# A self-check by four unsplit fp32 products and four transpositions, put into the projection stage of a transformer block

## The chip, the cores and the metric

The kernel runs on one core of a Trainium2 chip. The metric is the device time of one execution in microseconds (us); several executions are timed, and their median is compared. One execution of each kernel is also recorded by the profiler, instruction by instruction.

## The reference

One token sequence of 2048 rows by 576 features goes through a windowed attention and a mixer with an MLP, both under a modulated layer norm:

```python
mod = (_silu(c) @ w_mod).reshape(c.shape[0], 6, 1, -1)
sa, ca, ga, sb, cb, gb = (mod[:, i] for i in range(6))
h = _layernorm(x) * (1 + ca) + sa
x = x + ga * A_ref(h, A_wqkv, A_wo)      # 32 heads of 18, window of 256 rows, causal
h = _layernorm(x) * (1 + cb) + sb
x = x + gb * B_ref(h, B_w1, B_w2, B_w3, B_w4)
# B_ref: x1 = h + shifted(gelu(layernorm(h) @ w1)) @ w2
#        x1 + gelu(layernorm(x1) @ w3) @ w4, inner width 4608
```

All inputs and the output are fp32.

## The kernel before

The rows stand in 16 tiles of 128. The work goes through four stages: the projections to queries, keys and values (`qkv`), the attention with its output projection, the shifting mixer, and the MLP, which takes the rows in two halves of eight tiles (`sb`) and the inner width in blocks (`jj`).

Nearly all matrix products are done in split form: an fp32 operand is written as a high part in the type fp32r and a low remainder, and three fp32r products stand for one. A few products take fp32 operands as they are; here they are called unsplit. Those before the attention are the modulation vectors: `mod01` (L177) and `modr` (L194).

The order of all work is written out by hand. Each piece is put on a list with `at(t, f)`, where t is a planned time; at the end the list is sorted by t and the pieces are issued in that order. Each engine then runs its own instructions in just this order, and waits where an operand or a buffer isn't there yet. So a planned time fixes only the order, not the time.

In `qkv` the planned time starts at `T0` = 0 and the rows are taken in four groups of four tiles (b = 0 to 3), each planned for 47 us. For each group come nine blocks of query and key columns (`fmm`, L279, evacuated by `fev`, L284 on ScalarE and L285 on VectorE, stored by `fst`), then eight of values (`vmm`, L309, evacuated by `vev`, L314 on ScalarE and L315 on VectorE, stored by `vst`, L320). Between the value blocks of group b the normalised rows of group b + 1 are transposed in five steps k (`tr`, L254, four transpositions of 128x128 each); `hev` then scales them from PSUM into a buffer `hf` on VectorE (L259), rounds them to the high part on ScalarE (L261) and takes the remainder on GpSimd (L262). In group 0 also `modr(k)` runs on TensorE, with its sum `modre` on VectorE (L199, L201).

PSUM is used by named buffers of one each. `tr` alternates between `m0` (k even) and `m1` (k odd); `modr` uses `m1`; `fmm` and `vmm` go round `s0` to `s3`. A new tile of a name waits until the readers of the tile before it are done:

```python
pt = X["pt", b, k] = ps.tile([P, 512], F32, tag=f"m{k % 2}", name=f"pt{b}_{k}")
```

Around the planned time 30.5 the list reads: `vmm(0, 0)` 29.25, `fev(0, 8)` 29.35, `modr(2)` 30, `tr(1, 0)` 31, `vmm(0, 1)` 31.2, `vev(0, 0)` 31.3, `modre(2)` 31.5, `hev(1, 0)` 31.6.

At the end of the MLP each output tile is summed up in `acc[t]` by `dev` (L1175, VectorE), eight tiles in the order 4, 5, 6, 7, 0, 1, 2, 3, while TensorE computes the next tile (`run`, L1167) into the other one of two PSUM buffers; after the last block the tile is stored (L1178).

Of the kernel before, what the change touches and what calls it, by code (L numbers as in the profile page):

```python
# [8 lines left out]
F32 = mybir.dt.float32  # L9
# [3 lines left out]
ALU = mybir.AluOpType  # L13
# [6 lines left out]
P = 128  # L20
# [13 lines left out]
class Kern:  # L34
# [8 lines left out]
    def setup(self, stack):  # L43
        nc, tc = self.nc, self.tc
        self.ev = []
        self.cst = stack.enter_context(tc.tile_pool(name="cst", bufs=1))
        self.dr = stack.enter_context(tc.tile_pool(name="dr", bufs=1, space=DRAM))
        self.ps = stack.enter_context(tc.tile_pool(name="psU", bufs=1, space=PSUM))
        self.pools = {}
        c = self.cst  # L50
        self.ident = c.tile([P, P], F32, name="ident")
        self.identr = c.tile([P, P], F32R, name="identr")
        self.gb = c.tile([P, D], F32, name="gb")
        self.mhalf = c.tile([P, 1], F32, name="mhalf")
        self.rowm = c.tile([P, 8], F32, name="rowm")
        self.Mq = c.tile([P, 2, 64], F32R, name="Mq")
        self.Mk = c.tile([P, 5, 64], F32R, name="Mk")
        self.md = c.tile([P, 10], F32, name="md")
        self.qd = [self.dr.tile([2, D, 512], F32, name=f"qd{g}") for g in range(4)]
        self.kd = [self.dr.tile([2, D, 768], F32, name=f"kd{g}") for g in range(4)]  # L60
        self.vd = [self.dr.tile([P, VW], F32, name=f"vd{t}") for t in range(NT)]
        self.od = [self.dr.tile([512, D], F32, name=f"od{g}") for g in range(4)]
        self.xp = [self.dr.tile([P, D], F32, name=f"xp{t}") for t in range(NT)]
        self.hbd = [self.dr.tile([P, D], F32, name=f"hbd{t}") for t in range(NT)]
        self.xnd = [self.dr.tile([P, D], F32, name=f"xnd{t}") for t in range(NT)]
        self.modd = {v: self.dr.tile([1, D], F32, name=f"modd{v}") for v in (2, 3, 4, 5)}

    def at(self, t, f, *a):
        self.ev.append((t, (lambda: f(*a)) if a else f))
# [58 lines left out]
    def qkv(self, T0, TB):  # L128
        nc, at, ps = self.nc, self.at, self.ps
        X = {}  # L130
        at(-99, lambda: (self.open("qa", "left"), self.open("qb", "right")))
        qb = lambda *a, **k: self.pool_("qb").tile(*a, **k)
# [186 lines left out]
        def vst(t):  # L319
            nc.sync.dma_start(self.vd[t], X["Vst"][t % 3])  # L320

        at(-90, cond)
        for i in range(2):
            at(-89 + i, xload, i)
# [21 lines left out]
        for b in range(4):  # L346
# [7 lines left out]
            for i in range(4):  # L354
                t = 4 * b + i
# [16 lines left out]
            if b < 3:  # L372
                for i in range(4):
                    t = 4 * b + 4 + i
# [584 lines left out]
    def mlp(self):  # L959
        nc, ps, ident = self.nc, self.ps, self.ident  # L960
        NJ = F // 2 // P
        SB = S // 1024
        A, W3, W4, acc, gb = [], [], {}, {}, self.gb
# [15 lines left out]
        if True:  # L979
# [191 lines left out]
            def dev(jj, sb, t, last):  # L1171
                def f():
                    po = up_b[jj, "d", t][:, :, 0:288]
                    a = acc[t].rearrange("p (h d) -> p h d", h=2)
                    nc.vector.tensor_tensor(out=a, in0=po, in1=a, op=ALU.add)  # L1175
                    if last:
                        tt = 8 * sb + t
                        nc.sync.dma_start(self.out[tt * P:(tt + 1) * P, :], acc[t])  # L1178
                return f

# [126 lines left out]
```

## Time and profile before

| | |
|---|---|
| timed runs | 1858.69, 1849.98, 1856.75 us; median 1856.75 us |
| the profiled execution | 1853.12 us, its span 1851.3 us |
| TensorE multiplying | 1725.0 us (93% of the span) |
| VectorE / GpSimd / ScalarE | 1093.2 / 903.9 / 706.9 us |
| mean granted TensorE clock | 0.976 |

The span runs from the first to the last instruction; the execution's own time is 1.8 us longer. In the profile PE is TensorE multiplying, PEld TensorE loading the stationary operand, DVE VectorE, ACT ScalarE, POOL GpSimd, and SP the engine that issues the transfers. A row such as `L254 PE MATMUL pt<-ident,xh` gives the line, the engine, the operation, the written buffer and the read ones.

### The profile page before, as it was taken

How to read it: one execution, taken by the hardware profiler on the slowest of the kernel's cores; microseconds unless marked ns; L12 is line 12 of the kernel's file. 1: busy time of each engine (PE TensorE's matmuls, PEld its weight loads, DVE VectorE, ACT ScalarE, POOL GpSimd, SP SyncE). 2: the span in 40 equal slices, each digit the busy share in tenths (PEclk: the TensorE clock that was granted, in tenths of full speed). 3: DMA queues.
4: the chain of work that ended last, by engine and by line, in shares of the span. 5: the costliest groups of instructions: out<-in, count | busy, mean ns of one | idle time of the engine just before them, and what ended most of it. 6: DMA issues, size and time to landing. Idle time of an engine off the chain costs nothing.

```text
span 1851.3 us, 33769 instructions
## 1 busy us (share of the span) xinstructions
PE 1725.0 (93%) x13496; PEld 1572.3 (85%) x13496; DVE 1093.2 (59%) x1801; ACT 706.9 (38%) x1210; POOL 903.9 (49%) x842
## 2 busy tenths in 40 slices
PE   7999989889999998998779999999989999999998
PEld 6788878788888887998768899999978999999997
DVE  4644244465656562757556666666676666666664
ACT  2322134344444445344333333333343333333331
POOL 4322264445454533355576655555563655555550
PEclk9999979899999999999999999999989999999999
DMA  4955552444544535664442222222114222222211
GB/s 147 322 175 181 166 154 82 122 120 132 155 138 140 149 105 154 203 201 155 144 137 60 60 61 61 60 61 60 58 60 126 60 61 60 60 61 61 60 44 52
DMA packets 156420, 206.78 MB, mean 112 GB/s; under 512 B 19300, under 2 KB 87908, under 8 KB 155688
## 3 DMA queue, kind: packets, MB, share of 16 engines
q1 hardware_dynamic: 156264, 204.64, 36.1%
q8 instruction: 106, 1.74, 0.4%
q14 instruction: 50, 0.41, 0.1%
HBM read 143.76 MB, written 60.56 MB: 110 GB/s over the span
## 4 chain that ended last, share of the span: by engine, by line
PE 74%; DVE 7%; DMA 6%; POOL 5%; issue 3%; ACT 3%; SPq 2%; POOLq 0%; DVEq 0%; ACTq 0%
PE d L1167 23%; PE qk L279 6%; PE av L526 4%; PE v L309 3%; PE mx L444 3%; PE wo L611 3%; PE pg L828 3%; PE X L487 3%; DMA QD<-qd 2%; PE w L877 2%; DVE m L456 1%; PE X L489 1%; PE pm L177 1%; PE ot L536 1%; DVE W L1025 1%
## 5 line engine op out<-in xcount | busy, mean ns | idle before, releaser
L1167 PE MATMUL d<-W,G 128*128 128x288 f32 x3456 | 508.5, 298 | 16.3 <-DVE acc L1175 12.3
L1167 PEld LDWEIGHTS d<-W,G 128*128 128x128 f32 x3456 | 490.2, 190 | 38.3 <-DVE acc L1175 13.7
L1175 DVE TENSOR_TENSOR acc<-d,acc 128x576 f32<-128x576 f32 x288 | 216.6, 753 | 200.6 <-PE d L1167 198.4
L1005 POOL TENSOR_TENSOR wf<-wf 128x384 f32<-128x384 f32 x140 | 146.4, 1067 | 343.0 <-DMA wf<-in_B_w_dram 321.7
L456 DVE TENSOR_REDUCE m<-mx 128x2 f32<-128x640 f32 x224 | 181.2, 817 | 159.6 <-PE mx L446 157.4
L504 ACT ACTIVATE P<-X 128x512 f32<-128x512 f32 (+4 forms) x320 | 180.5, 573 | 207.2 <-PE X L489 204.5
L444 PE MATMUL mx<-KD,QS 128*128 128x320 f32 (+4 forms) x512 | 157.6, 358 | 37.8 <-POOL QS L427 22.5
L427 POOL TENSOR_SCALAR QS<-QD,rowm 128x512 fp32r<-128x512 f32 x128 | 87.9, 699 | 142.2 <-DMA QD<-qd 70.2
L487 PE MATMUL X<-QD,KS 128*128 128x64 f32 (+2 forms) x704 | 151.6, 307 | 3.7 <-ACT P L504 3.2
L1144 DVE TENSOR_TENSOR G<-U,G 128x512 fp32r<-128x512 f32 x108 | 95.3, 882 | 99.8 <-ACT G L1137 99.8
L1017 POOL TENSOR_TENSOR W<-wf,W 128x768 fp32r<-128x768 f32 x70 | 152.0, 2193 | 1.2 <-ACT W L1011 1.2
L444 PEld LDWEIGHTS mx<-KD,QS 128*128 128x128 f32 x512 | 102.0, 199 | 45.4 <-POOL QS L427 23.8
L1135 ACT ACTIVATE U<-U 128x512 f32<-128x512 f32 x108 | 68.3, 632 | 179.3 <-DVE U L1120 179.3
L1135 ACT ACTIVATE C<-C 128x512 f32<-128x512 f32 x36 | 22.8, 632 | 285.9 <-DVE C L1120 285.9
L279 PE MATMUL qk<-hT,Wqk 128*128 128x512 f32 x504 | 120.9, 401 | 0.0
L279 PEld LDWEIGHTS qk<-hT,Wqk 128*128 128x128 f32 x504 | 95.8, 191 | 24.2 <-issue 0.9
L487 PEld LDWEIGHTS X<-QD,KS 128*128 128x128 f32 x704 | 106.7, 195 | 10.6 <-ACT P L504 7.8
L434 POOL TENSOR_SCALAR KS<-KD,rowm 128x768 fp32r<-128x768 f32 (+1 forms) x128 | 107.6, 853 | 0.0
L1031 POOL TENSOR_TENSOR wf<-wf,gb 128x1152 f32<-128x1152 f32 x35 | 103.4, 2955 | 7.1 <-DMA wf<-in_B_w_dram 7.1
L446 PE MATMUL mx<-Mq,identr 128*128 128x128 f32 x448 | 101.5, 227 | 0.0
L1046 POOL TENSOR_TENSOR W<-wf,W 128x1152 fp32r<-128x1152 f32 x35 | 96.7, 2762 | 6.9 <-ACT W L1040 6.9
L1011 ACT CAST W<-wf 128x1152 fp32r<-128x1152 f32 x70 | 90.2, 1318 | 21.9 <-DMA wf<-in_B_w_dram 11.2
(765 smaller groups left out, 3198.0 us busy)
## 6 DMA issues: line engine op xcount, KB each, us to landing
wf<-in_B_w_dram SPq DMA_DIRECT2D x35, 576.0 KB
wf<-in_B_w_dram SPq DMA_DIRECT2D x140, 128.0 KB
KD<-kd SPq DMA_DIRECT2D x72, 216.0 KB
QD<-qd SPq DMA_DIRECT2D x96, 144.0 KB
wf<-in_B_w_dram SPq DMA_DIRECT2D x140, 64.0 KB
qd<-qs SPq DMA_DIRECT2D x16, 512.0 KB
kd<-qs SPq DMA_DIRECT2D x16, 512.0 KB
vd<-Vst SPq DMA_DIRECT2D x16, 312.0 KB
```

The source lines that it names most:

```text
L279: nc.tensor.matmul(po, W[:, a, fs], H[:, c, :], start=(n == 0), stop=(n == 13))
L434: nc.gpsimd.tensor_scalar(t[:, b0:, r], src[:, b0:], M[:, 2 + r:3 + r], 0.0, op0=ALU.mult, op1=ALU.add)
L444: nc.tensor.matmul(pm[:, s, 320 - 64 * nb:320], lhs, K[:, j, 64 * (i + 5 - nb):64 * (i + 5)], start=True, stop=False)
L446: nc.tensor.matmul(pm[:, s, 0:320].rearrange("p (a b) -> p a b", b=64)[:, 0::4, :], self.identr, self.Mq, start=False, stop=True)
L456: nc.vector.tensor_reduce(out=m[:, c:c + 2], in_=pm[:, :, 0:320], axis=mybir.AxisListType.X, op=ALU.max, negate=True)
L487: nc.tensor.matmul(px[:, c:c + q1 - q0], K[:, b + 4].rearrange("p r k -> p (r k)"), Q[:, j, q0:q1], start=(i == 0), stop=False)
L504: nc.scalar.activation(p[:, lo:], X["px", n, j, k][:, lo:], AF.Exp, scale=SCALE)
L1005: nc.gpsimd.tensor_tensor(out=WF[:, o], in0=WF[:, a], in1=WF[:, b], op=ALU.subtract)
L1017: eng.tensor_tensor(out=W[:, s0:s1, 3:5, :], in0=WF[:, 1 + s0:1 + s1, 0:2], in1=W[:, s0:s1, 0:2, :].bitcast(F32), op=ALU.subtract)
L1031: nc.gpsimd.tensor_tensor(out=R4, in0=R4, in1=gb.unsqueeze(1).to_broadcast([P, 2, D]), op=ALU.mult)
L1167: nc.tensor.matmul(po, G[:, g, ta, b, ts], W[:, w, b, cs], start=(n == 0), stop=(n == 5))
L1175: nc.vector.tensor_tensor(out=a, in0=po, in1=a, op=ALU.add)
```

## The change

A function `resid` is put on the list at 30.5. It takes the input rows of tile 4 (`X["x", 4]`, loaded earlier for the layer norm), 512 of their 576 columns. Four unsplit fp32 products load 128 columns of the rows each as the stationary operand and stream the identity; their result in PSUM (`m0`) is copied to a buffer of `hf` by ScalarE. Then four plain transpositions of the same columns go to a new tile of `m0`, and VectorE takes the difference, multiplies it by a million, squares it and sums it up over the columns into `res`, one number for each partition. In the MLP `res` is added to the output rows of tile 8 before they are stored. One constant buffer of 4 bytes a partition is new. Nothing is removed or moved.

```diff
+        self.res = c.tile([P, 1], F32, name="res")
...
+        def resid():
+            x = X["x", 4]
+            pp = ps.tile([P, 512], F32, tag="m0", name="rp")
+            for k in range(4):
+                nc.tensor.matmul(pp[:, k * P:(k + 1) * P], x[:, k * P:(k + 1) * P], self.ident, start=True, stop=True)
+            d = qb([P, 512], F32, tag="hf", name="rd", bufs=2)
+            nc.scalar.copy(d, pp)
+            pp = ps.tile([P, 512], F32, tag="m0", name="rp2")
+            for k in range(4):
+                nc.tensor.transpose(pp[:, k * P:(k + 1) * P], x[:, k * P:(k + 1) * P], self.ident)
+            nc.vector.tensor_tensor(out=d, in0=pp, in1=d, op=ALU.subtract)
+            nc.vector.tensor_scalar(d, d, 1e6, None, op0=ALU.mult)
+            nc.vector.tensor_tensor(out=d, in0=d, in1=d, op=ALU.mult)
+            nc.vector.tensor_reduce(out=self.res, in_=d, axis=mybir.AxisListType.X, op=ALU.add)
+
+        at(T0 + 30.5, resid)
...
                     if last:
                         tt = 8 * sb + t
+                        if tt == 8:
+                            nc.vector.tensor_scalar(acc[t], acc[t], self.res, None, op0=ALU.add)
                         nc.sync.dma_start(self.out[tt * P:(tt + 1) * P, :], acc[t])
```

## The prediction

> **What bounds the kernel now.** I read the page first, for the engine that carries the chain of work.
>
> ```profile
> span 1851.3 us, 33769 instructions
> ...
> PE 74%; DVE 7%; DMA 6%; POOL 5%; issue 3%; ACT 3%; SPq 2%; POOLq 0%; DVEq 0%; ACTq 0%
> ```
>
> TensorE carries three quarters of the chain that ended last. An average says little about one place, so next come the busy times in stretches of the projection stage and TensorE's waits from 40 to 205 us.
>
> ```profile
> 80.00:100.00 20.00, 19.82 (x149) 16.92 (x148) 9.12 (x15) 5.70 (x13) 6.43 (x5) 1.00 0.54 182
> ...
> 160.00:200.00 40.00, 40.00 (x232) 35.57 (x231) 16.80 (x32) 10.85 (x24) 8.78 (x11) 1.00 0.45 154
> ```
>
> ```profile
> PE pmr L194 <- DMA wm<-in_w_mod_dram: 1.4, 1, 1.4
> PE pt L254 <- DVE macc L201: 0.2, 1, 0.2
> ```
>
> The second number of a row is TensorE's busy time: 19.82 of 20 us, later 40.00 of 40. In these 165 us it waited 1.6 us in all, the 1.4 us of it ahead of L194's first use. So nothing in this stage would take up a delay of TensorE; a microsecond that it loses behind the new code is a microsecond by which the stage ends later. The third view is the timeline where the new code goes in, between `modr(2)` (L194) and `tr(1, 0)` (L254).
>
> ```profile
> 75.74 1.18 PE L194 MATMUL pmr<-wm,silub 128*32 128x288 f32 x16
> ...
> 76.71 0.39 ACT L314 COPY Vst<-v 64x288 f32<-64x288 f32 x1
> ...
> 76.85 0.69 DVE L285 TENSOR_TENSOR qs<-qk,qs 128x512 fp32r<-128x512 f32 x1 [1.15 <-ACT qs L284]
> 76.85 0.66 PE L254 MATMUL pt<-ident,xh 128*128 128x128 f32 x4
> ...
> 77.26 3.95 PE L309 MATMUL v<-Wv,hT 128*128 128x288 f32 x28
> 77.57 0.46 DVE L315 COPY Vst<-v 64x288 f32<-64x288 f32 x1
> ...
> 78.06 0.76 DVE L201 TENSOR_TENSOR macc<-pmr,macc 128x576 f32<-128x576 f32 x1
> 78.73 0.80 DVE L259 TENSOR_SCALAR hf<-pt,md 128x512 f32<-128x512 f32 x1
> 79.57 0.62 ACT L261 CAST hT<-hf 128x512 fp32r<-128x512 f32 x1 [2.46 <-DVE hf L259]
> 80.21 0.39 ACT L314 COPY Vst<-v 64x288 f32<-64x288 f32 x1
> 80.64 0.46 DVE L315 COPY Vst<-v 64x288 f32<-64x288 f32 x1 [1.10 <-ACT Vst L314]
> 81.05 0.60 PE L254 MATMUL pt<-ident,xh 128*128 128x128 f32 x4
> ```
>
> The reader is to see that TensorE goes from one group to the next without a pause, that a group of four transpositions takes 0.60 to 0.66 us, and that the evacuations hand over within 0.02 to 0.06 us (79.53 to 79.57, 79.57 + 0.62 to 80.21).
>
> **The change part by part.** Nothing is removed or moved; every term is an addition. The prices of single instructions, as min/median/max where three numbers stand:
>
> ```profile
> 10.04 20.98 PE L177 MATMUL pm<-silu,wm 128*128 128x1 f32 x100 [10.04 <-DVE rowm L108]
> ...
> L177 PE MATMUL pm<-silu,wm x100: 242/352/371, 10.0 to 30.8; 128*128 128x1 f32 x64, 128*64 128x1 f32 x16, 64*128 64x1 f32 x16, 64*64 64x1 f32 x4
> ...
> L194 PE MATMUL pmr<-wm,silub x80: 402/406/431, 58.2 to 94.7; 128*32 128x288 f32 x64, 64*32 64x288 f32 x16
> ...
> L254 PE MATMUL pt<-ident,xh x80: 270/272/477, 30.9 to 184.1; 128*128 128x128 f32 x80
> ...
> L531 ACT COPY avs<-av x32: 573/594/616, 285.8 to 725.5; 128x512 f32<-128x512 f32 x32
> ...
> L246 DVE TENSOR_SCALAR xh<-x,a7mv,a7rs x1: 579/579/579, 73.6 to 73.6; 128x576 f32<-128x576 f32 x1
> ...
> L456 DVE TENSOR_REDUCE m<-mx x224: 769/823/826, 235.4 to 694.7; 128x2 f32<-128x640 f32 x112
> ```
>
> (1) The four products. `modr` has 40 products and `mod01` 50, and the rows show 80 and 100 records: an unsplit product is two records, so this is 8. The trace has none with 128 loaded and 128 streamed columns. Least: the spacing of the transpositions, which load and stream the same shapes, (0.60 - 0.27) / 3 = 0.11 us, so 7 x 0.11 + 0.27 = 1.04 us. Most: the spacing of L177, 20.98 / 100 = 0.21 us, and L194's 0.41 for the last: 1.88 us. L177 ran early, when TensorE was slower: its 352 ns for one streamed column is more than L254's later 272 for 128. So I stay nearer the low end, at L309's spacing (28 in 3.95, 0.14 us, a full load beside a stream), with 0.35 for the last: 7 x 0.14 + 0.35 = 1.33 us. The records of L194 and L177 show how many instructions there are, not how often each streams. [...]
>
> (2) The new waits on TensorE. The second `m0` tile can't be written until ScalarE has copied the first, so TensorE stands still: handover 0.04, copy 0.59 (L531, same shape), handover 0.06. ScalarE is free by then (its L314 ends at 77.10, the products end at 76.85 + 1.33 = 78.18). Then four transpositions, 0.66. Then `tr(1, 0)` wants `m0` a third time and waits for the subtraction: handover 0.04, 0.69 (L285: two operands, one in PSUM, 512 columns), handover 0.06. Sum 0.69 + 0.66 + 0.79 = 2.14 us, all on the path, because behind these instructions in TensorE's queue stands the whole rest of the stage.
>
> (3) VectorE's other three. Scaling 0.58 (L246, at most), squaring 0.69 (L285's), summing 0.65 (L456: 0.82 for 640 columns, here 512): 1.92 us in front of L315, L201 and L259, which stood right behind. `hev(1, 0)` started 1.88 us after `tr(1, 0)`; now it starts after 1.86 + 0.46 + 0.76 and two handovers, 3.13 us: 1.25 us later against TensorE. The first `tr` on `m1` needs L201's end (3.1 us after `tr(1, 0)`) and comes 4.20 us after it (81.05 - 76.85), so it doesn't wait. What is late next shows in the chain of waits ten microseconds further:
>
> ```profile
> 84.07 0.82 DVE hf L259
> ...
> 84.91 0.62 ACT hT L261
> ...
> 85.56 0.40 ACT Vst L314
> ...
> 85.98 0.46 DVE Vst L315
> ...
> 86.47 0.77 DVE macc L201
> ...
> 87.29 0.66 PE pt L254 x4
> ```
>
> This chain from VectorE and ScalarE already ends 0.2 us after TensorE asked for `m1`. Following `hev`, rounding and value copies one by one behind the late start (each L259, L261, L314, L315 in the order of the list, with the rows' durations), the delay shrinks from 1.25 to 0.66 us at `hev(1, 1)`, and L201 ends 11.0 us after `tr(1, 0)` where it ended 10.4 us after it: 0.6 us more of waiting. Bounds: 0 if the idle gaps before L259 take it up, 1.25 if none is made up.
>
> (4) Other queues. SP issues no new transfer. The store of the first value tile waits for L315 and goes out some 5 us later; behind it in SP's queue stand only stores of the next value tiles, and their reader is the attention, 140 us on. GpSimd gets nothing, and its work on `hT` is late by the same time as TensorE. The rows of tile 4 get a reader more; the load that takes over their buffer belongs to the next group, planned at 50, and comes after the new code in any case.
>
> (5) The addition at the end, 0.58 us on VectorE by L246:
>
> ```profile
> 1842.78 0.76 DVE L1175 TENSOR_TENSOR acc<-d,acc 128x576 f32<-128x576 f32 x1 [0.84 <-PE d L1167]
> 1844.37 0.76 DVE L1175 TENSOR_TENSOR acc<-d,acc 128x576 f32<-128x576 f32 x1 [0.84 <-PE d L1167]
> ```
>
> The tile is the fifth of the last eight (1842.78). Behind it VectorE is idle for 0.84 us until TensorE has the next tile, and the PSUM buffer is already free, so 0.58 us fits: nothing. If VectorE took over 0.84 us, the next tile would be late by the excess, and three more gaps of 0.84 us would make it up.
>
> Sum: 1.33 + 2.14 + 0.6 = 4.1 us; with all low ends 1.04 + 2.14 = 3.2, with all high ends 1.88 + 2.14 + 1.25 = 5.3. Against the profiled execution: 1853.12 + 4.1 = 1857.2. That execution is 3.6 us under the median of the runs shown, and the four times together average 1854.6, so I forecast 1854.6 + 4.1 = 1858.7 us.
>
> **The rivals.** First, the granted clock drops behind the new waits. Two stretches speak to it:
>
> ```profile
> 56.00:58.20 2.20, 0.80 (x4) 0.33 (x3) 2.20 (x2) 0.61 (x2) 2.20 (x2) 1.00 0.95 366
> 58.20:60.00 1.80, 1.79 (x19) 1.07 (x20) 0.22 (x1) 0.00 (x0) 0.05 (x1) 1.00 1.06 408
> 226.50:228.40 1.90, 0.28 (x3) 0.04 (x1) 0.00 (x0) 0.39 (x1) 1.38 (x3) 1.00 0.84 280
> ...
> 231.00:232.00 1.00, 1.00 (x7) 1.00 (x6) 0.00 (x0) 0.39 (x1) 0.00 (x0) 0.50 0.61 150
> ...
> 229.00:235.00 6.00, 6.00 (x36) 6.00 (x36) 2.03 (x6) 0.44 (x2) 1.92 (x4) 0.72 0.49 143
> ```
>
> TensorE idled 1.4 us ahead of 58.2 and kept its clock of 1.00; it idled 1.6 us ahead of 228.4 and then got 0.72 over six microseconds, a loss of 6 x 0.28 = 1.7 us. [...] If it drops, the time is 4.1 + 1.7 = 5.8 us up, 1860.4. [...]
>
> Second, on the slower side: that low clock stays until the next `fmm`, because the stretch from 81 to 95 is broken up by transpositions and by narrow products. Its 14 us at half the clock would add 14 us, and the time would be 1873. It decides from 9.3 - 4.1 = 5.2 us on, that is over 10 us at half clock. Against it stands that 229 to 235 was broken up in the same way and had its clock back within 6 us.
>
> Third, the delay is made up later: the attention begins with waits for transfers, and what TensorE lost might be time that it would wait there. Then the time is 1854.6, no change. Against it: the first loads of the attention reuse buffers that TensorE's last projections free, so they are late by the same time.
>
> Fourth, that the unsplit products are not what they say: were they one record each like a transposition, 4 x 0.14 us less, 1858.1; it changes nothing that can be measured.
>
> **How the numbers follow.** Apart by 0.5%, or 9.3 us, is about what a measurement of this kernel can tell from no change, since its own runs lie 8.7 us apart. Chances: the forecast 0.45, the lower clock for 6 us 0.30, made up later 0.13, the clock low until 95 us 0.05, and 0.07 for something that no row prices, such as the buffers behind the new 4-byte constant coming to lie elsewhere, with a gain (0.03) as likely as a loss (0.04). The first three lie within 0.5%, except where the scatter of the runs carries the first two over 1866 (0.05 of their 0.75). So slower 0.05 + 0.04 + 0.05 = 0.14, faster 0.03, same 0.83. The range reaches from 1851 (made up later, runs like the lower ones) to 1867 (lower clock on runs like the highest, 1858.69 + 5.8 = 1864.5, and a little for the high price of the products).
>
> **What the next profile would show.** Eight records of the products at about 0.14 us; two idle gaps of TensorE of about 0.7 and 0.8 us, released by ScalarE's copy and by VectorE's subtraction; `tr(1, 0)` 3.5 us after the place where it stands now; the wait of L254 for L201 grown from 0.2 to about 0.8 us; the last `fmm` of the stage about 4 us later and the distance from it to the end unchanged; at the end VectorE's gap after the fifth tile down from 0.84 to some 0.3 us. The forecast is wrong if the stage ends much later than that, if the clock in the stretch from 80 to 95 is under 1.00, or if the later stages give time back.

## The result and the profile after

The changed kernel takes 1868.62 us (median of six executions, 1862.07 to 1870.72) against 1854.47 us for the kernel before (six executions): a ratio of 1.0072, interval 1.005 to 1.0093. The same kernel in a later set, twelve executions, had 1.0048, interval 1.0031 to 1.0066 (f1 below). So it is slower by 9 to 14 us where 4.1 were forecast, and the first median lies over the top of the range. The difference between the two sets is as large as the forecast cost itself; no run here explains it.

The profiled execution took 1868.91 us. Its page begins:

```profile
span 1867.1 us, 33796 instructions
...
PE 1728.8 (93%) x13508; PEld 1571.6 (84%) x13508; DVE 1096.1 (59%) x1806; ACT 707.5 (38%) x1211; POOL 904.4 (48%) x842
```

TensorE multiplies 3.8 us longer than before (1725.0) in a span that is 15.8 us longer: most of the loss is waiting or the place of work, not work.

The new code itself behaves as forecast. The next view is the timeline of the profiled execution after; its lines are 17 further down than before behind the new function, and one above it.

```profile
79.11 1.16 PE L327 MATMUL rp<-ident,x 128*128 128x128 f32 x8
...
80.36 0.59 ACT L329 COPY rd<-rp 128x512 f32<-128x512 f32 x1 [2.91 <-PE rp L327]
...
81.00 0.66 PE L332 MATMUL rp<-ident,x 128*128 128x128 f32 x4 [0.73 <-ACT rd L329]
81.77 0.69 DVE L333 TENSOR_TENSOR rd<-rp,rd 128x512 f32<-128x512 f32 x1 [3.59 <-PE rp L332]
...
82.51 0.66 PE L255 MATMUL pt<-ident,xh 128*128 128x128 f32 x4 [0.86 <-DVE rd L333]
...
93.45 0.65 PE L255 MATMUL pt<-ident,xh 128*128 128x128 f32 x4 [0.68 <-DVE macc L202]
```

Eight records of the products in 1.16 us; 0.73 us of waiting for ScalarE's copy; the transpositions; 0.86 us of waiting for VectorE's subtraction; `tr(1, 0)` at 82.51, which is 3.40 us after the place 79.11 where it would have stood. The later `tr(1, 3)`, on `m1`, waits 0.68 us for L202 instead of the 0.2 us before. The waits of TensorE in the whole stage, 40 to 205 us, have nothing else that is new:

```profile
PE pmr L195 <- DMA wm<-in_w_mod_dram: 2.3, 1, 2.3
PE pt L255 <- DVE rd L333: 0.9, 1, 0.9
PE rp L332 <- ACT rd L329: 0.7, 1, 0.7
PE pt L255 <- DVE macc L202: 0.7, 1, 0.7
```

The first row is a transfer that comes before the new code, and 0.9 us more than before. TensorE comes to L195 at 78.00 us, 2.3 us later than in the profile of before (75.74). That isn't the change: in the nine profiles of the first timing and the first two sets below it comes there 0.4 to 4.4 us later than in before's one, in e2 and e4 too, which have no new code (0.4 and 2.0). The busy times by stretch, with the granted clock in the third column from the end:

```profile
74.00:95.00 21.00, 18.74 (x148) 15.97 (x147) 10.94 (x17) 5.14 (x11) 4.07 (x4) 1.00 0.65 237
...
160.00:200.00 40.00, 40.00 (x232) 35.41 (x232) 18.36 (x36) 10.95 (x24) 9.62 (x13) 1.00 0.45 155
```

TensorE is busy 18.74 of 21 us where the new code lies, at a mean clock of 1.00, and 40.00 of 40 later. At the end VectorE's addition (L1196) fits into its gap: 0.84 us, then 0.28, then 0.83.

```profile
1858.58 0.76 DVE L1192 TENSOR_TENSOR acc<-d,acc 128x576 f32<-128x576 f32 x1 [0.84 <-PE d L1184]
1859.38 0.52 DVE L1196 TENSOR_SCALAR acc<-acc,res 128x576 f32<-128x576 f32 x1
1860.18 0.76 DVE L1192 TENSOR_TENSOR acc<-d,acc 128x576 f32<-128x576 f32 x1 [0.28 <-PE d L1184]
1861.77 0.76 DVE L1192 TENSOR_TENSOR acc<-d,acc 128x576 f32<-128x576 f32 x1 [0.83 <-PE d L1184]
```

So from the new code up to 95 us and in the last ten microseconds all is as forecast, and the missing 5 to 10 us lie in between, in stages whose code is untouched. When equal instructions of the two profiles are laid side by side, the difference (after less before) is 6.2 us, constant, from 92 to 222 us: 3.9 us of the change and the 2.3 that were lost ahead of it. Then it is 11.6 at 407, 9.8 at 705, 12.9 at 750, 15.7 at 850 and 15.8 at the end. Which of these steps belong to the change, one pair of profiles can't tell.

### The profile page after: what moved, and what is told of

Its sections match the earlier page's. It is cut to its first block, busy times and chain, and to the rows that moved or that the text cites. A ratio compares the mean times of both kernels' runs of the same rounds, so it can differ in the third digit from the quotient of the medians.

```text
span 1867.1 us, 33796 instructions
## 1 busy us (share of the span) xinstructions
PE 1728.8 (93%) x13508; PEld 1571.6 (84%) x13508; DVE 1096.1 (59%) x1806; ACT 707.5 (38%) x1211; POOL 904.4 (48%) x842
## 3 DMA queue, kind: packets, MB, share of 16 engines
q8 instruction: 106, 1.74, 0.4%
## 4 chain that ended last, share of the span: by engine, by line
PE 58%; DVE 7%; issue 3%; ACT 3%; DMA 3%; POOL 2%; SPq 1%; POOLq 0%; DVEq 0%; ACTq 0%
PE d L1184 23%; PE av L543 3%; PE pg L845 3%; PE wo L628 3%; PE mx L461 2%; PE w L894 2%; PE X L504 2%; DMA QD<-qd 1%; DVE W L1042 1%; DMA wf<-in_B_w_dram 1%; DVE m L473 1%; PE X L506 1%; PE ot L553 1%; DVE U L1137 1%; PE u4P L1131 1%
```

## Experiments

The executions of one kernel scatter more than the effect (before's 31 in the last set lie 16.5 us apart, 1846.31 to 1862.84), so each kernel below the first row was timed in five rounds beside the kernel before. Four sets (e, f, h, g) were run, each on one chip. "Stop" is explained behind the second set: how many `av` products TensorE has still to do when it stops near the end of the attention. "Excess" is the mean of the kernel's executions less the mean of those of before in the same set, with its standard error.

| kernel | new code | stop (products left) | buffers moved | ratio, interval | excess us |
|---|---|---|---|---|---|
| the change, first timing | yes | 33 | yes | 1.0072, 1.005 to 1.0093 | 13.8 ± 2.0 |
| e1 | yes | 33 | no | 1.003, 1.0014 to 1.0046 | 4.8 ± 1.0 |
| e2 | no | 21 | yes | 1.000, 0.998 to 1.0019 | -0.4 ± 1.4 |
| e3 | yes | 33 | yes | 1.0049, 1.0028 to 1.007 | 8.8 ± 1.3 |
| e4 | no | 21 | yes | 1.0029, 1.0012 to 1.0046 | 3.8 ± 1.1 |
| f1, the change again | yes | 33 | yes | 1.0048, 1.0031 to 1.0066 | 8.9 ± 1.3 |
| f2 | yes | 33 | to 256 B | 1.0039, 1.0022 to 1.0057 | 7.7 ± 1.3 |
| f3 | yes, other banks | 33 | yes | 1.0049, 1.0032 to 1.0067 | 8.4 ± 1.1 |
| f4 | a plain delay | 49 | yes | 1.0056, 1.0034 to 1.0079 | 11.6 ± 1.8 |
| h1 | no | 33 | no | 1.0011, 0.9995 to 1.0027 | 1.9 ± 1.1 |
| h4 | no | 13 | no | 1.0003, 0.9985 to 1.0021 | 1.3 ± 1.5 |
| h2 | yes | 21 | yes | 1.0031, 1.0014 to 1.0048 | 5.6 ± 1.3 |
| h3 | yes | 21 | no | 1.0028, 1.0014 to 1.0043 | 5.1 ± 1.1 |
| g1 (as h2) | yes | 21 | yes | 1.0031, 1.0017 to 1.0046 | 6.8 ± 1.0 |
| g2 | yes | 33 | yes | 1.0058, 1.0034 to 1.0081 | 10.9 ± 1.5 |
| g3 (as h3) | yes | 21 | no | 1.0028, 1.0011 to 1.0045 | 6.1 ± 1.2 |
| g4 | yes | 33 | no | 1.0039, 1.0021 to 1.0057 | 7.6 ± 1.4 |

**First set: is it the 4-byte constant?** In the compiled program the new constant `res` takes 32 bytes a partition and moves the pools behind it by that much; `QD` and `KD`, the buffers that the attention loads, started at multiples of 256 bytes before and no longer do. Four kernels part this from the new code.

```diff
e1: the whole change, the result in a free column of an older constant
-        self.res = c.tile([P, 1], F32, name="res")
+        self.res = self.rowm[:, 6:7]
e2: before, with an unused constant; e4: the same with 16 columns
+        self.pad = c.tile([P, 1], F32, name="pad")
+        at(T0 + 30.5, lambda: nc.gpsimd.memset(self.pad, 0.0))
e3: the whole change, the constant 64 bytes
+        self.res16 = c.tile([P, 16], F32, name="res")
+        self.res = self.res16[:, 0:1]
```

> The whole change, but res lies in an unused column of the buffer rowm, so that no new constant exists and every buffer of the attention, mixer and MLP lies at the address of the kernel before. Theory A (placement: the new constant moves these buffers by 32 bytes, their loads get slower, and about 10 of the 14 us come from there; the delay of TensorE in the projections is the other 4): 3 to 5 us over the kernel before, packets of 3072 bytes in the attention back from 193 to about 176 ns. Theory B (the delay of 4 us shifts the later stages against their transfers, and waits grow from that): 12 to 16 us over the kernel before, as the changed kernel. Theory C (the later differences are scatter between executions): 3 to 5 us, but then the next kernel is at 0.

> The kernel before with nothing but an unused constant of 4 bytes a partition, which takes 32 bytes of room and is set once by GpSimd while that is idle. Theory A: 7 to 12 us slower than the kernel before, packets of 3072 bytes in the attention at about 193 ns. Theories B and C: 0, within 2 us, packets at 176 ns.

> The whole change with the new constant made 64 bytes a partition: the same buffers move by 64 bytes in place of 32, so they start at multiples of 64 as in the kernel before. Theory A in the form that the remainder by 64 counts: 3 to 5 us over the kernel before. Theory A in the form that any other address costs: 12 to 16 us. Theory B: 12 to 16 us. Theory C: 3 to 5 us.

> The kernel before with an unused constant of 64 bytes a partition. Theory A by the remainder by 64: 0, within 2 us. Theory A by any shift: 7 to 12 us slower. Theories B and C: 0.

The move alone (e2) costs nothing that can be seen, e4's 64 bytes 3.8 us; the change without the move (e1) still costs 4.8. So the move isn't the main cause. The results of e3 (8.8) and e4 (3.8) lie between what the three theories expected, so none of the three is right alone. The move does show in the transfers. In the queue view from 420 to 600 us the last three numbers of a row are packets, megabytes and the share of 16 engines' time: before, then e2, then e1.

```profile
q1 hardware_dynamic: 15237, 24.87, 47.8%
```

```profile
q1 hardware_dynamic: 15010, 24.19, 48.4%
```

```profile
q1 hardware_dynamic: 15267, 24.43, 47.0%
```

Share by megabyte is 1.92 before and in e1 (47.0 / 24.43), 2.00 in e2: packets of the moved buffers take longer. Among the 3072-byte ones (the loads of `KD`) the median is 161 ns before, 162 in e1, 182 in e2. No run here shows what in such a packet takes the longer time.

**Second set: the move again, and the delay by itself.** f1 is the change unaltered. f2 makes the constant 256 bytes, so the buffers lie at multiples of 256 again. f3 takes TensorE's two waits away by giving products and transpositions a bank each (`s0`, `s1`). f4 has neither products of the rows nor the end addition; it only holds TensorE for 4 us in the same place.

```diff
f2
+        self.res64 = c.tile([P, 64], F32, name="res")
+        self.res = self.res64[:, 0:1]
f3
-            pp = ps.tile([P, 512], F32, tag="m0", name="rp")
+            pp = ps.tile([P, 512], F32, tag="s0", name="rp")
...
+            p2 = ps.tile([P, 512], F32, tag="s1", name="rp2")
f4, in place of the body of resid
+            for k in range(28):
+                nc.tensor.matmul(pp[:, 0:288], H[:, k % 4, 0:P], Wv..., start=(k == 0), stop=(k == 27))
+            nc.vector.tensor_copy(self.res, pp[:, 0:1])
```

> The changed kernel once more, beside the next three. It is here for its median and a second profile. If the 13 us of its first runs belong to the kernel: 12 to 16 us over the kernel before. If they came from the chip of that day: 4 to 8 us over it, like the version with res in rowm (4.5 us). The local cost between the last narrow product ahead of the new code and the next group of query products: 3.9 us again.

> The whole change with the new constant made 256 bytes a partition, so the later buffers move by 256 bytes. In the kernel before the attention's load targets start at multiples of 256 bytes, and moves by 32 and by 64 bytes both lengthened their 3072-byte packets (medians 182 and 179 ns against 161). Theory D (the start by 256 bytes sets the packet time, and slower loads cost time only together with the delay): packets back at about 161 ns, 3 to 6 us over the kernel before, some 8 us under the changed kernel. Theory B (the delay alone): as the changed kernel, and packets without influence. Theory C (scatter that has nothing to do with placement): anything from 3 to 14 us, with packets at 161 or 182 ns alike.

> The whole change, but the products and the transpositions write two PSUM buffers that are free at that time (s0 and s1), and the copy by ScalarE comes after both, so TensorE waits for nobody. The steps of the prediction: of the 3.9 us the 2 us of waiting go, 1.2 + 0.45 us of work and some of the 0.5 us of VectorE's lateness stay, so the stage ends 1.7 to 2.2 us late. If the rest of the loss follows the delay (theory B or D): under 8 us over the kernel before. If it has another cause in the new code: still about 12 us.

> In place of the check 28 ordinary split products of a value block, 3.95 us of TensorE's time without a wait, into the same PSUM buffer, and one copy of a column to res; nothing is added to the output. The constant of 4 bytes stays, with its move by 32 bytes. Theories B and D (delay, with or without the placement): 10 to 16 us over the kernel before, as the changed kernel. If the unsplit products, the waits or the addition at the end matter by themselves: 3 to 6 us.

f1's 8.9 us lie between the 4 to 8 expected of scatter and the 12 to 16 expected of the kernel. f2's packets are as short as before (1.91 by the same rows: 46.7 / 24.50), and it costs 7.7 us, where 3 to 6 were expected if the packets decided. f3 shows 3.1 us at 95 us, where 1.7 to 2.2 were expected: TensorE's two waits are gone, but `tr(1, 3)` then waits 1.4 us for VectorE's sum (L202). It costs 8.4 us in all; f4 shows 4.2 us at 95 us and costs 11.6. So neither the move nor the form of the local code is the key: what adds TensorE work in this set costs more than it takes on the spot. f4 left two explanations standing: a later start at 82 us costs more than itself, or something that products added ahead change further on.

**What the traces then showed.** In every profile TensorE stops once between 720 and 740 us, in the last group of `av` products (L526 in before), with nothing that the profile shows it to wait for. These are the kernel before and the changed one, ScalarE's row first or second by time:

```profile
721.44 0.62 ACT L761 CAST W<-w1r 128x512 fp32r<-128x512 f32 x1 [3.89 <-DMA xmt<-xnd]
...
722.88 0.53 PE L526 MATMUL av<-P,V 64*32 64x128 f32 x21 [1.36 <-issue]
...
725.04 1.05 ACT L531 COPY avs<-av 128x512 f32<-128x512 f32 x2
...
727.36 2.74 PE L611 MATMUL wo<-Wo,T 128*128 128x288 f32 x14 [2.16 <-DVE T L599]
```

```profile
732.86 0.65 PE L543 MATMUL av<-P,V 64*32 64x192 f32 x33 [1.88 <-issue]
...
733.26 0.62 ACT L778 CAST W<-w1r 128x512 fp32r<-128x512 f32 x1 [6.07 <-PE av L543]
...
736.86 1.05 ACT L548 COPY avs<-av 128x512 f32<-128x512 f32 x2
...
739.31 3.38 PEld L628 LDWEIGHTS wo<-Wo,T 128*128 128x128 f32 x14 [4.25 <-DVE T L616]
```

The bracket is the idle time before the row and what ended it. Before, the stop (1.36 us) has 21 `av` products behind it; after, it (1.88 us) has 33. Of TensorE's product records 6793 lie ahead of the stop in both, and in all kernels of the first two sets: the place belongs to the stream of instructions, not to a piece of the program, and the twelve records added at 79 us move it twelve products back. The rows of queue 8 fit that:

```profile
q8 instruction: 106, 1.74, 0.4%
```

1.74 MB in 106 packets is 16 KB a packet; one of them moves at 720.4 us in the kernel before, ahead of the resumption at 722.88. In all 18 profiles such a packet begins 2.3 to 2.7 us ahead of the resumption, whether the stop is 0.45 or 3.54 us long; it is the queue's 53rd, and the 54th where 116 or more products are added early (the third and fourth sets). TensorE's 13496 product records over the 106 packets are 127 to a packet, and the 6793 over 53 are 128. So a packet carries, by an estimate from these counts, about 128 products with their weight loads, and the next such place should lie 128 products later; the next sets test that. That the stop is a wait for this packet is an inference from these numbers, and why this packet comes so late stays open. In before, at the other places that lie a multiple of 128 products from this one, TensorE's records follow one another without a gap; here there is one of 1.36 us.

Why twelve products matter: ScalarE's first cast of the mixer weights (L761) waits for a product of the last `av` group. In all 18 profiles one ends 0.06 to 0.07 us before that cast starts; in the kernel before a transfer to `xmt` lands at the same time, and the row names that one. With 21 left, the product is done ahead of the stop, and the ten casts start beside it. With 33 left it lies behind the stop, the casts start after it, and ScalarE's copy of `av`, which the first `wo` product needs in the end, stands behind the casts. This is theory E.

**Third set: move the stop alone.** Small products are issued in the first 10 us, where TensorE waits for the first loads (its first product starts at 10.04 us in before), and they move no buffer. (The expectations below put the stops so far at 1.4 to 3.5 us; f2's was 0.45.)

```diff
h1: before, n = 12; h4: before, n = 120; h2: the change, n = 116; h3: e1, n = 116
+        def idle():
+            t = ps.tile([P, 512], F32, tag="s0", name="idle")
+            for k in range(n):
+                nc.tensor.matmul(t[0:32, 0:32], self.identr[0:32, 0:32], self.identr[0:32, 0:32], start=True, stop=True)
+        at(-96.5, idle)
```

> The kernel before, with twelve small products of 32 columns put on TensorE before 10 us, where it waits for the first loads, so nothing is delayed by them. Their output is used by nothing. In every run so far TensorE stops for 1.4 to 3.5 us, with nothing waited for, ahead of product record 6793, near 722 us; twelve added records move that stop twelve products back in the program. Theory E (the stop): it falls with 33 products of the last group of L526 still to come instead of 21, ScalarE's first cast of the mixer weights then waits for products behind the stop and starts near 726 instead of 722, the first wo product waits about 4 us instead of 2, and the time rises by 3 us (1 to 5) over before, ratio 1.0005 to 1.0027. Theories of place (no buffer is moved) and of delay (nothing is later at 82 us): 0 (-1.5 to 1.5 us).

> The same with 120 small products before 10 us: ten times the added work, still ahead of the first loads. Theory E: the stop, if it stays at a fixed count of records, moves 120 products back, and the next one, 128 products later in the stream, comes 8 products later than in before, so 13 products of the last group of L526 are left behind it; the cast starts ahead of it, and the time is that of before, 0 (-2 to 1.5 us). If the early products themselves cost time, this kernel is slower than the one with twelve.

> The changed kernel with 116 small products before 10 us, which with the change's own twelve records make 128. Theory E: the stop falls with 21 products left, as in before; the wo wait is 2 us or less again, and of the change's cost what is left is the 3.9 us at 78 to 95 us and 0 to 3 us of the moved buffers: 4 to 6.5 us over before, ratio 1.002 to 1.0035, against 9 us (f1) of the changed kernel alone. Theory of delay (a later start at 82 us costs more than itself further on, whatever the stream): 9 us as f1.

> The same 116 products with the change whose result lies in a free column of an older constant, so no buffer moves. Theory E: the 3.9 us at 78 to 95 us and nothing else, 3 to 5 us over before, and 1 to 3 us below the changed kernel without moved buffers of the first set (4.5 us over before). If the stop costs nothing in the end, the same as that kernel, 4.5 us; if the moved buffers cost something, the other kernel of 128 lies above this one by 1 to 3 us.

The stop went where it was expected: to 33, 13, 21 and 21 products left. h1 and h4 in the same rows:

```profile
724.44 0.65 PE L532 MATMUL av<-P,V 64*32 64x192 f32 x33 [2.64 <-issue]
...
724.84 0.62 ACT L767 CAST W<-w1r 128x512 fp32r<-128x512 f32 x1 [6.83 <-PE av L532]
...
728.44 1.06 ACT L537 COPY avs<-av 128x512 f32<-128x512 f32 x2
...
730.89 3.38 PEld L617 LDWEIGHTS wo<-Wo,T 128*128 128x128 f32 x14 [3.35 <-DVE T L605]
```

```profile
726.82 0.62 ACT L767 CAST W<-w1r 128x512 fp32r<-128x512 f32 x1 [3.89 <-PE av L532]
...
728.47 0.34 PE L532 MATMUL av<-P,V 64*32 64x64 f32 x13 [1.52 <-issue]
...
730.42 1.05 ACT L537 COPY avs<-av 128x512 f32<-128x512 f32 x2
...
732.74 2.48 PEld L617 LDWEIGHTS wo<-Wo,T 128*128 128x128 f32 x14 [2.38 <-DVE T L605]
```

Twelve idle products at the start of the program put the casts behind the stop (6.83 us idle instead of 3.89); 120 put them ahead of it again. Measured from the end of ScalarE's work before the casts, `wo` starts 9.81 us later in before (727.36 - 721.44 + 3.89) and in h4, 12.88 in h1, 12.12 in the change. Over all 18 profiles of this study: 9.81 us in seven and 10.11 in one of the eight with 21 or 13 products left; in the ten with 33 or 49 left 10.70 to 14.22, each time the length of the stop (0.45 to 3.54) and 10.2 to 10.7 us. The mean of the ten is 12.2, so on the spot the change of place costs 2.4 us. The clock pays as well; it is the third number from the end, 731 to 738 us, in h1 and in e2, whose stops end about 0.2 us apart:

```profile
731.00:738.00 7.00, 7.00 (x38) 6.98 (x39) 3.46 (x10) 1.61 (x4) 3.86 (x5) 0.65 0.07 20
```

```profile
731.00:738.00 7.00, 7.00 (x59) 7.00 (x58) 3.18 (x9) 4.11 (x8) 4.47 (x6) 1.00 0.51 153
```

These two are near the ends: h4, with 13 products left, has 0.76 in the same stretch. In the 14 us behind the resumption the mean clock is 0.88 to 1.00 in the eight profiles with 21 or 13 products left (0.88 in before) and 0.54 to 0.88 in the ten others.

In the total the set says less: 1.9 ± 1.1 us for h1 against 1.3 ± 1.5 for h4, which can't be told apart; h2 and h3 lie at 5.6 and 5.1, in reach of the forecast's 4.1. But h3 was expected 1 to 3 us below e1, the same change with the stop at 33, and e1 had 4.8 on another chip; taken alone that speaks for a stop that costs nothing in the end.

**Fourth set: two by two on one chip.** The change and e1, each with 116 or 128 early products (stop at 21 or at 33), so that the early work differs by twelve small products only.

```diff
g1: the change, g3: e1, both as h2 and h3
+            for k in range(116):
g2: the change, g4: e1
+            for k in range(128):
```

> The changed kernel with 116 small early products, as in the set before, now on one chip with the next three. With the change's twelve records the stop of TensorE lies 21 products ahead of the end of the last L526 group. Theory E: clock 1.00 at 724 to 731 us and a wo wait of 1.5 us, and 3.3 us (1 to 5) less than the kernel with 128 early products. Placement: 1 to 3 us more than the kernel with 116 and no moved buffers.

> The changed kernel with 128 small early products, all before 10 us: twelve more than its neighbour, with nothing else different. A whole block of 128 products and loads is added, so that the stop is again 33 products ahead of the end of the L526 group, as in the change itself. Theory E: first cast about 4 us later behind the last P tile, wo wait 3 to 4 us, a granted clock well under 1 between 724 and 738 us, and 3.3 us (1 to 5) more than with 116. If the place of the stop costs nothing in the end: the same to 1 us.

> The change without moved buffers and with 116 early products: stop at 21. Both theories (stop and moved buffers) make it the fastest of the four, 4 us (3 to 5) over before: the 3.9 us at 78 to 95 us alone. If a start 3.9 us later at 82 us costs more by itself: 7 us or more.

> The change without moved buffers and with 128 early products: stop at 33. Theory E: 3.3 us (1 to 5) over the one with 116. Moved buffers: 1 to 3 us below the kernel with 128 and moved buffers. If neither, all four lie within 1 us of one another.

TensorE's waits near the stop, in g1 and then g2:

```profile
PE av L549 <- issue: 2.5, 1, 2.5
```

```profile
PE wo L634 <- DVE T L622: 4.0, 1, 4.0
PE av L549 <- issue: 2.0, 1, 2.0
```

With the stop at 33 `wo` waits 4.0 us for `T` in g2, and 4.0 in g4; with the stop at 21 it waits 1.5 in g3, and in g1 no such wait shows. (The clock that was expected of g2 from 724 to 738 us, well under 1, didn't show there: it was 0.97, since the resumption came only at 732.05 us; in the 14 us behind it the clock was 0.76, against 0.88 in g1.) In time, the pair with moved buffers differs by 0.0027 of the ratio (5 us; by means 4.0 ± 1.6), the pair without by 0.0011 (2 us; 1.5 ± 1.6). The means over both pairs give the stop 2.7 ± 1.1 us and the move 2.0 ± 1.1. g3, expected 4 us over before, came out at 6.1 ± 1.2.

A least-squares fit to the excess of all kernels of the table but f4 (sixteen values; f2 counted as not moved), one price for each of the columns, gives 4.9 ± 0.6 us for the new code, 2.0 ± 0.6 for the stop and 2.2 ± 0.6 for the moved buffers. Their sum, 9.1, is f1's excess (8.9). The weighted squares of what is left sum to 21 at 13 degrees of freedom: somewhat more scatter than the standard errors give; the first timing's 13.8 us is a quarter of it. Values of one set share the runs of before; fitted with a baseline for each set, the three prices are 4.7, 2.3 and 2.1 us.

## Why the prediction was wrong

**The terms of the sum** held, one by one. (1) Products: 1.33 forecast, 1.16 measured, the spacing that of the transpositions (0.11 us). The records show two for a product; how often each of them streams, no run here shows. (2) Waits and transpositions: `tr(1, 0)` 3.47 later forecast, 3.40 measured (0.73 and 0.86 us of waiting for 0.69 and 0.79). (3) The later wait on `m1`: 0.6 more forecast, 0.5 measured. (5) The end: the gap of 0.84 became 0.28, forecast 0.3. Sum 4.1 forecast, 3.9 on the spot, and 4.9 ± 0.6 in the total by the fit.

**The step that failed** is that of the next profile, "the distance from it to the end unchanged", and with it step (4), "Other queues": it asked who waits for the delayed work, not what the added instructions do to the streams further on. Two terms of about 2 us each were missing. The twelve records moved a stop that TensorE makes anyway from beside ten casts to in front of them; this is shown by the time at which `wo` starts in h1, where twelve idle products alone do it, and in g1 against g2 (10.11 and 12.20 us). Its price is 2.4 us on the spot, 2.0 ± 0.6 in the fit and 2.7 ± 1.1 in the two by two; in the total it rests on these averages, since h1 and h4 alone don't part. And the new constant moved the buffers, where the prediction has "Nothing is removed or moved", for 2.2 ± 0.6 us in the fit. This second one the prediction had named, "the buffers behind the new 4-byte constant coming to lie elsewhere", with 0.07 and either sign; it was put at nothing in the sum, though e2 alone shows none of it. That the moved buffers cost time in the total rests on the fit (the two by two gives 2.0 ± 1.1). Where it is spent isn't settled. From 312 to 407 us, early in the attention, the profiles with moved buffers lost 1.8 ± 0.3 us against before (ten), the others 0.2 ± 0.5 (seven), which is a hint.

**The rivals.** The granted clock didn't drop at the new waits: it was 1.00 from 74 to 95 us, with pauses of 0.73 and 0.86 us, shorter than the 1.4 us ahead of 58.2 us that left it at 1.00 in before. So neither the first nor the second rival came about; that transpositions and narrow products would have held a low clock down was the author's guess, and no run shows it. The clock did drop further on, near the `wo` wait, in before too (0.83 from 724 to 731 us) and lower with the stop at 33 (0.65 in h1 from 731 to 738 us). That the delay is made up later fell: with stop and buffers as before (h3, g3) the cost was 5.1 and 6.1 us. That the products are one record each fell with the eight records.

**The range** took the scatter of before's runs, and had the rest of the kernel as a rigid block. By the fit's sum the change is 1854.5 + 9.1 = 1863.6 us, inside it, but by luck: the room was left for a lower clock that didn't come; the remaining 5 us of the first timing (13.8 against 8.9 in f1, the same kernel) stay open. Of the profile pair's 15.8 us not all is the change's: 2.3 were lost ahead of the new code, and the 2.5 from 828 to 850 us are in most profiles (0.8 to 2.5 in 16 of 17, h1 and h4 among them, which add nothing but early products; 0.2 in e2), so there the one profile of before was a quick one.

## What to carry to other kernels

In this kernel, with an in-order list on each engine, the edit cost its local price (4.9 ± 0.6 us in the fit) and what it shifted: the addresses of the buffers allocated behind a new tile (2.2 ± 0.6) and the place where an instruction stream pauses (2.0 ± 0.6). Put small constants into free columns of older ones (e1, 4.8 us over before, against 8.8 and 8.9 in e3 and f1), and when a change of a few microseconds costs twice its price, lay equal instructions of both traces side by side and look for a wait "issue" whose count of instructions, not whose place in the program, is the same. Idle instructions where the engine waits anyway move such a pause back and price it: with 116 early products the changed kernel was 5.6 (h2) and 6.8 us (g1) over before, against 8.9 without (f1).

## What the runs showed that was not expected

- TensorE stopped for 0.45 to 3.54 us at a fixed count of its records (6793, or 128 later when 116 to 128 products are added). In the seven microseconds ahead of the resumption the transfers took 0.74 (g3) to 0.97 (before) of the DMA engines' time.
- With the loaded buffers moved by 32 bytes off a multiple of 256 (e2), 3072-byte packets were 13% longer (161 to 182 ns) and the queue's time for each megabyte 4% longer (1.92 to 2.00); moved by 256 bytes (f2), that time was 1.91.
- An unsplit fp32 product of 128 by 128 by 128 cost two records at 0.11 us each, the spacing of plain transpositions.
